# Opening of an attention and phase-mixing kernel: side work of batch 0 and the scores of batch 1 are held until batch 0's sines are rounded

## The chip, the core and the metric

The kernel runs on one core of a Trainium2 chip. Five engines work side by side, each with its own queue of instructions in a fixed order: TensorE (PE, matrix products into PSUM), VectorE (DVE), ScalarE (ACT), GpSimd (POOL) and SyncE (SP), which here issues the DMAs. They wait for each other through semaphores. The metric is the device time of one execution in microseconds, the median of several runs. The time before is 597.99 us.

## The reference

Eight batches go through a masked attention and then through a layer that mixes positions and channels:

```python
scores = scale * np.matmul(q, k.transpose(0, 1, 3, 2))
scores = np.where(masks[None, :, :, :], scores, -1000000000.0)
attn = softmax(scores)                     # with 1e-9 in the divisor
x = concat_heads(np.matmul(attn, v))       # (8, 576, 512)
theta = x @ w_theta
zr, zi = x * np.cos(theta), x * np.sin(theta)
y = einsum('ts,bsd->btd', w_tok_r, zr) + einsum('ts,bsd->btd', w_tok_i, zi)
u = x + y
out = u + np.maximum(u @ w_ch, 0.0)
```

There are 8 heads of width 64 and 576 positions. Half of the heads look back over a window of 32 positions, the other half over every fourth of 128 positions. The weight matrices are shared by all batches.

## The kernel before

**What is computed in which form.** Heads are taken in four pairs per batch, (b, pr). Since each query sees few keys, the scores of a pair are nine blocks of 128 x 64 (`scores`, L438), made by 36 small matmuls in two groups of PSUM bank `s`, which has two buffers. The softmax runs along the 64 columns: DVE takes maxima, ACT takes exponentials, POOL multiplies by the reciprocal of the sum (L507). The matrix P (two buffers from batch 1 on) is transposed in `turn` (L511, eight DVE instructions a pair) and multiplied with V in `pv` (L600). V comes in two parts, `va` with two buffers and `vb` with one.

Large products are made from rounded halves: a float is split into a high part (a cast, on ACT or DVE) and a low part (a subtraction on POOL), and three products of halves replace one. That holds for the weights (`split`, L344), for x (`x_split`), for the products with sine and cosine (`zsplit`, L630; names `zh`, `zl`) and for u (`residual`, L774). The weights come from the host as 64-bit words and are unpacked first (`unpack`, L308: a clamp on DVE, two passes on ACT of which one may go to DVE, and a combination on DVE).

**The stages of a batch.** `theta` makes five tiles of 128 rows of theta (the last, with 64 rows, first), `trig` (L722) turns each into sine and cosine, multiplies with x and rounds, which gives nine pairs `zh`, `zl` (NK = 9). `token` (L790) adds nine times three products with the token weights; there are 4 x 2 such units, first those with weights g = 0 (`wtkh`, `wtkl`, loaded early), then g = 1 (`late_wt_a`, `late_wt_b`, the late token weights). `chan` (L821) does the channel product, another eight units.

**The order.** From batch 1 on, `phase` (L841) interleaves the units of one batch with the scores, products and theta of the next by a table. The opening, from the loads of batch 0 to the end of its units, is written by a planner instead (class `Order`). Each piece of work is a generator that yields an engine with a cost, or an event to wait for; the planner keeps a clock for each engine and gives a free engine to the ready piece with the lowest rank (`RANK`, L33). The order in which the pieces come out is the order of instructions in each engine's queue, and it is fixed (`pin`). The events of the planner only shape that order; what an instruction really waits for on the chip is its data and its buffers.

The pieces that matter here: `theta_split` (L358) splits the theta weights, which batch 0 uses whole and batch 1 in halves; `token_weights(1, n, ...)` (L365) unpacks and splits the five late token weights, in buffers (`u3`, `xh0` to `xh3`) that are free between other uses; `chan_weights` (L381) does so for the channel weights, in `xh2` and `xh3` after them; `scores(1, pr)` are the scores of batch 1, of which pairs 2 and 3 wait for the event `sin0` (all sines and cosines of batch 0 have been taken). Exponential and sine need different tables of ACT, so a change between them loads a table.

`on_pe` (L412) says for which pairs the mask is added by PE (a matmul of a bf16 identity with the mask, `mask_on_pe`); then DVE takes row maxima of the masked scores (`row_max`) and ACT takes exponentials straight from PSUM (L482). For the others, among them pairs 0 and 1 of batch 1, DVE adds the mask and takes the maximum in nine instructions (`mask_scores`, L406), writing the masked scores to P, and ACT takes exponentials from there (L501).

Of the kernel before, what the change touches and what calls it, by code (L numbers as in the profile page):

```python
# [30 lines left out]
LATE = ("u3", "xh1", "xh2", "xh3", "xh0")  # L31
LATE2 = ("xh2", "xh3", "xh2", "xh3")
RANK = dict(load=6.64, scores0=1.09, flip=0.01, pv0=1.13, pair=.21, theta_unpack=1.54, theta0=5.3, trig0=2.41,  # L33
            token_early=2.55, theta_split=6.42, token_late=6.75, chan=2.1, units=2.95, evacuate=4.49,
            scores1=4.02, scores2=7.3, pv1=8.0, theta1=5.96, trig1=7.42)
STS = (4, 0, 1, 2, 3)

# [14 lines left out]
NK = 9  # L52
# [7 lines left out]
class Order:  # L60
# [13 lines left out]
    def pin(self, ins):  # L74
        if self.live:
            self.tc.keep_in_program_order(ins)

    def signal(self, event):
        self.events[event] = self.now

    def go(self, gen, rank=None):
        if not self.live:
            for _ in gen:
                pass
            return
        self.serial += 1
        t = [self.rank if rank is None else rank, self.serial, self.now, gen, None, 0.0]
        self.tasks.append(t)
        self.advance(t)
# [39 lines left out]
def dve(n):  # L129
    return 67 + 1.04 * n  # L130


def dve2(n):
    return 67 + 0.52 * n


def act(n):
    return 95 + 0.83 * n
# [6 lines left out]
def dma(n):  # L145
    return 128 * 4 * n / 360.0
# [3 lines left out]
def build(ctx, tc, qT, kT, vw, wth, wtk, wch, maskb, ident, identb, outT):  # L150
# [14 lines left out]
    pin, go, signal = od.pin, od.go, od.signal  # L165

    def pe(ins):
        tc.keep_in_program_order(ins)
# [17 lines left out]
    def take(tag, bufs, n=None):  # L186
        n = reserve(tag) if n is None else n
        if od.live:
            if n >= bufs:
                yield None, ("free", tag, n - bufs)  # L190
            if n:
                yield None, ("got", tag, n - 1)
            signal(("got", tag, n))
        return n
# [113 lines left out]
    def unpack(src, sz, name, stage, early, n, key):  # L308

        tag = None  # L310
        if stage is None:
            st = hp.tile([128, 2 * DM], F32R, tag=f"wc{n}", name=f"st_{name}{n}")
        else:
            tag = stage
            yield from take(tag[0], 1, tag[1])
            st = hp.tile([128, 2, S], F32R, tag=tag[0], name=f"st_{name}{n}").rearrange("p a b -> p (a b)")
        raw = st[:, :2 * sz].bitcast(U32)
        yield "DMA", dma(2 * sz)
        if len(src.shape) == 3:
            pin(nc.sync.dma_start(raw.rearrange("p (c b) -> p c b", c=src.shape[1]), src.bitcast(U32)))  # L320
        else:
            pin(nc.sync.dma_start(raw, src.bitcast(U32)))
        signal(("raw", name, n))
        yield None, ("raw", name, n)
        pair = raw.rearrange("p (a b) -> p a b", b=2)
        Ci, Ti = pair[:, :, 1], pair[:, :, 0]
        C, T = Ci.bitcast(F32), Ti.bitcast(F32)
        yield "DVE", dve2(sz)
        pin(nc.vector.tensor_scalar(C, C, W_MAX, -W_MAX, op0=ALU.min, op1=ALU.max))
        yield "ACT", act(sz)  # L330
        pin(nc.scalar.activation(C, C, AF.Prelu, scale=2.0 ** -112, alpha=-2.0 ** 32))
        if early and n % 2 == 0:
            yield "DVE", dve2(sz)
            pin(nc.vector.tensor_scalar(Ti, Ti, 29, None, op0=ALU.logical_shift_right))
        else:
            yield "ACT", act(sz)
            pin(nc.scalar.activation(Ti, Ti, AF.Copy, scale=2.0 ** -29, bias=-0.5))
        yield "DVE", dve(sz)
        pin(nc.vector.scalar_tensor_tensor(out=Ti, in0=Ci, scalar=3, in1=Ti,
                                           op0=ALU.logical_shift_left, op1=ALU.bitwise_or))  # L340
        signal(key)
        return T, tag
# [15 lines left out]
    def theta_split(c):  # L358
        for st in range(5):
            yield None, ("th0", st, c)  # L360
        wths[c] = tuple(cp.tile([128, DM], F32R, name=f"wth{h}{c}") for h in "hl")
        yield from split(wth32[c], DM, wths[c], ("wth", c))
        signal(("wc", c))
# [46 lines left out]
        signal(key)  # L410

    def on_pe(b, pr):  # L412
        return b == 0 or (b, pr) in ((1, 2), (1, 3), (2, 0), (2, 1))

    def mask_on_pe(ps, pr, g0, g1):
        n = g0
# [20 lines left out]

    def scores(b, pr):  # L438
        yield None, ("qk", b, pr)
        if b == 1 and on_pe(b, pr):  # L440
            yield None, "sin0"
        if pr >= 1:
            yield None, ("sc", b, pr - 1)
        q, k, rqk = qks[b, pr]
        if b == 0:
            P, rp = pqs[pr].rearrange("p (a b) -> p a b", b=BW), None
        else:
            rp = yield from take("P", 2)
            P = sp.tile([128, NJ, BW], F32, tag="P", name=f"P{b}_{pr}")
        mx = sp.tile([128, NJ], F32, tag=f"mx{b == 0 and pr}", name=f"mx{b}_{pr}", bufs=1 if b == 0 else 2)  # L450
        sm = sp.tile([128, NJ], F32, tag=f"sm{b == 0 and pr}", name=f"sm{b}_{pr}", bufs=1 if b == 0 else 2)
        held = {}
        for g0, g1 in ((0, 5), (5, NJ)):
            ps, rel = yield from bank("s", f"s{b}_{pr}_{g0}")
            ps = ps[:, :(g1 - g0) * BW].rearrange("p (a b) -> p a b", b=BW)
            held[g0] = ps, rel
            masked = on_pe(b, pr)
            if masked:
                yield "PE", 150
                mask_on_pe(ps, pr, g0, g1)  # L460
            yield "PE", 162 * (g1 - g0)
            for n in range(g0, g1):
                for e in range(2):
                    qb = 2 * n + e
                    pe(nc.tensor.matmul(ps[64 * e:64 * e + 64, n - g0], q[:, qb],  # L465
                                        k[:, QB * qb:QB * qb + BW], start=not masked, stop=not masked or n == g1 - 1))
            if masked:
                go(row_max(b, ps, rel, P, mx, g0, g1, ("mask", b, pr, g0)))
            else:
                go(mask_scores(ps, rel, P, mx, pr, g0, g1, ("mask", b, pr, g0)))  # L470
        signal(("sc", b, pr))
        if b == 0:
            give(f"u{pr}", 0)
        else:
            give("qk", rqk)
            go(load_qk(b * NP + pr + 2), RANK["load"])
        if b and on_pe(b, pr):
            for g0, (ps, rel) in held.items():
                yield None, ("mask", b, pr, g0)
                yield "ACT", 335 * ps.shape[1]  # L480
                for n in range(ps.shape[1]):
                    table(nc.scalar.activation(P[:, g0 + n], ps[:, n], AF.Exp, bias=mx[:, g0 + n:g0 + n + 1],  # L482
                                               scale=SCALE, accum_out=sm[:, g0 + n:g0 + n + 1]))
                give(*rel)
        else:
            for g0 in (0, 5):
                yield None, ("mask", b, pr, g0)
        if b == 0:
            yield "ACT", act(S)
            table(nc.scalar.activation(P, P, AF.Exp, scale=SCALE))  # L490
            yield "DVE", dve(S)
            pin(nc.vector.tensor_reduce(sm, P, op=ALU.add, axis=mybir.AxisListType.X))
        elif not on_pe(b, pr):
            yield "DVE", 67
            pin(nc.vector.tensor_scalar(mx, mx, -SCALE, None, op0=ALU.mult))  # L495
            if b == 1:
                yield None, "sin0"
            for n0 in range(0, NJ, 3):
                yield "ACT", 720
                for n in range(n0, n0 + 3):  # L500
                    table(nc.scalar.activation(P[:, n], P[:, n], AF.Exp, bias=mx[:, n:n + 1], scale=SCALE,  # L501
                                               accum_out=sm[:, n:n + 1]))
        yield "DVE", 200
        pin(nc.vector.tensor_scalar(sm, sm, 1e-9, None, op0=ALU.add))
        pin(nc.vector.reciprocal(sm, sm))
        yield "POOL", 1110
        pin(nc.gpsimd.tensor_tensor(P, P, sm.unsqueeze(2).to_broadcast([128, NJ, BW]), op=ALU.mult))  # L507
        probs[b, pr] = P, rp
        signal(("P", b, pr))
# [363 lines left out]
    def units(b):  # L873
        for f, i, g in UNITS:
            yield from f(b, i, g)

    def thetas(b):
        for st in STS:
            yield from theta(b, st)
            go(trig(b, st), RANK["trig1"])  # L880

    def sins(b):
        for st in STS:
            yield None, ("sin", b, st)
        signal("sin" + str(b))
# [33 lines left out]
    for n in range(NC):  # L919
        go(chan_weights(n, LA2[n]), RANK["chan"] + n * .01)  # L920
    go(sins(0), 0)
    go(units(0), RANK["units"])
    for p in range(NP):
        go(scores(1, p), RANK["scores1"] + p * RANK["pair"])
# [78 lines left out]
```

## Time and profile before

| | |
|---|---|
| runs, us | 596.26, 597.99, 598.92 (median 597.99) |
| profiled execution, us | 597.07 |
| its span, us | 595.3 |
| mean granted clock of PE | 0.984 |
| instructions | 14176 |
| DMA | 67.76 MB, mean 114 GB/s |

The span is the stretch from the first to the last instruction of the profiled execution; its time has a little around it. An engine's busy share is a mean over the span. A line of the timeline gives start, duration, engine, line of the kernel, operation, output and inputs, the number of merged instructions, and in brackets the time for which the engine was idle before it and what released it. A line of the groups gives the number of instructions, their busy time in us, the mean of one in ns, and the idle time before them.

Busy tenths of PE and of the clock that was granted to it, in 40 slices of the span:

```profile
PE   5997898999999999999999999999999999999997
PEclk9999599999999999999999999999999999999999
```

The page's two lines show an opening in which PE is not full, and from the sixth slice on a PE that nearly always has work.

### The profile page before, as it was taken

The numbers are of one execution on the slowest core, as the hardware profiler recorded it, in microseconds if no ns is written. First come the engines' busy times: TensorE is split into PE (matmuls) and PEld (weight loads), VectorE is DVE, ScalarE is ACT, GpSimd is POOL, SyncE is SP. The second block draws the span as 40 slices with busy tenths as digits, with TensorE's granted clock in tenths as the row PEclk, the third lists the DMA queues.
The fourth block names the chain that finished last, engine by engine and source line by source line (L and its number), as shares of the span: only waits on it lengthen the run. The fifth ranks groups of instructions, "written<-read, shape, count | busy, mean of one in ns | idle before, by whom it ended". The sixth has DMA issues, their size and how long they took to land.

```text
span 595.3 us, 14176 instructions
## 1 busy us (share of the span) xinstructions
PE 569.7 (96%) x5584; PEld 516.9 (87%) x5584; DVE 361.6 (61%) x1132; ACT 351.1 (59%) x939; POOL 222.4 (37%) x206
## 2 busy tenths in 40 slices
PE   5997898999999999999999999999999999999997
PEld 4744787979998899889998899989998899989997
DVE  3889888855765667465566567655665656445112
ACT  1498967687535955568553974468564785266110
POOL 2229854534322532326142442316324253315220
PEclk9999599999999999999999999999999999999999
DMA  8982347404650074302641054401742023001002
GB/s 303 398 339 61 121 160 246 142 1 141 182 160 3 2 241 142 101 2 89 197 139 62 1 181 151 154 1 40 231 142 73 0 81 100 1 1 53 28 1 81
DMA packets 26866, 67.76 MB, mean 114 GB/s; under 512 B 2992, under 2 KB 3248, under 8 KB 26800
## 3 DMA queue, kind: packets, MB, share of 16 engines
q1 hardware_dynamic: 26800, 66.86, 32.9%
q8 instruction: 44, 0.72, 0.5%
q14 instruction: 22, 0.18, 0.1%
HBM read 57.41 MB, written 9.44 MB: 112 GB/s over the span
## 4 chain that ended last, share of the span: by engine, by line
PE 49%; DVE 22%; ACT 21%; issue 3%; POOL 2%; DMA 2%; SPq 0%; ACTq 0%; DVEq 0%; POOLq 0%
PE y L804 27%; DVE pt L522 9%; PE c L834 8%; PE s L465 5%; ACT P L501 5%; PE o L614 4%; PE th L682 3%; ACT K L697 3%; ACT zh L641 3%; ACT g L754 2%; ACT K L695 2%; DVE P L406 2%; DVE K L702 2%; POOL P L507 2%; ACT L754 1%
## 5 line engine op out<-in xcount | busy, mean ns | idle before, releaser
L787 POOL TENSOR_TENSOR u<-x,u 128x288 fp32r<-128x288 f32 x64 | 54.9, 858 | 184.9 <-ACT u L785 162.2
L522 DVE STREAM_TRANSPOSE pt<-P 32x288 f32<-32x288 f32 x224 | 105.1, 469 | 21.1 <-POOL P L507 18.0
L834 PE MATMUL c<-u,late_wc 128*128 128x288 f32 x768 | 111.7, 296 | 0.8 <-DVE x L813 0.5
L834 PEld LDWEIGHTS c<-u,late_wc 128*128 128x128 f32 x768 | 106.2, 188 | 4.8 <-DVE x L813 2.0
L785 ACT CAST u<-x 128x288 fp32r<-128x288 f32 x64 | 27.5, 430 | 129.3 <-DVE x L782 129.3
L804 PE MATMUL y<-wtkh,zh 128*128 128x288 f32 x288 | 90.6, 315 | 1.1 <-ACT zh L641 1.1
L804 PE MATMUL y<-wtkh,zl 128*128 128x288 f32 x288 | 86.6, 301 | 3.7 <-POOL zl L643 3.7
L804 PE MATMUL y<-wtkl,zh 128*128 128x288 f32 x288 | 86.2, 299 | 0.0
L643 POOL TENSOR_TENSOR zl<-g,zh 128x512 fp32r<-128x512 f32 x40 | 52.6, 1316 | 79.1 <-ACT zh L641 66.7
L501 ACT ACTIVATE P<-P,mx 128x64 f32<-128x64 f32 x216 | 72.1, 336 | 16.8 <-DVE mx L495 16.8
L682 PE MATMUL th<-wthh,xh 128*128 128x512 f32 x224 | 76.3, 402 | 0.0
L782 DVE TENSOR_TENSOR x<-y,x 128x288 f32<-128x288 f32 x64 | 28.7, 450 | 66.8 <-PE y L804 64.0
L804 PE MATMUL y<-late_wt_b,zh 128*128 128x288 f32 x320 | 68.1, 297 | 0.0
L804 PE MATMUL y<-late_wt_a,zh 128*128 128x288 f32 x256 | 58.0, 308 | 2.7 <-DVE x L782 2.7
L804 PEld LDWEIGHTS y<-wtkh,zh 128*128 128x128 f32 x288 | 55.4, 192 | 4.8 <-ACT zh L641 2.3
L804 PEld LDWEIGHTS y<-wtkh,zl 128*128 128x128 f32 x288 | 55.3, 192 | 4.5 <-POOL zl L643 4.5
L804 PEld LDWEIGHTS y<-wtkl,zh 128*128 128x128 f32 x288 | 55.5, 193 | 0.3 <-issue 0.3
L643 POOL TENSOR_TENSOR zl<-K,zh 128x512 fp32r<-128x512 f32 x32 | 42.0, 1312 | 36.1 <-ACT zh L641 36.1
L507 POOL TENSOR_TENSOR P<-P,sm 128x576 f32<-128x576 f32 x32 | 37.5, 1172 | 43.8 <-ACT xh L590 19.3
L804 PEld LDWEIGHTS y<-late_wt_b,zh 128*128 128x128 f32 x320 | 51.4, 189 | 0.3
L682 PEld LDWEIGHTS th<-wthh,xh 128*128 128x128 f32 x224 | 42.1, 188 | 8.3
L804 PE MATMUL y<-late_wt_b,zl 128*128 128x288 f32 x160 | 47.3, 296 | 0.0
(103 smaller groups left out, 1110.0 us busy)
## 6 DMA issues: line engine op xcount, KB each, us to landing
q<-in_qT_dram SPq DMA_DIRECT2D x32, 576.0 KB, 4.2
va<-in_vw_dram SPq DMA_DIRECT2D x30, 320.0 KB, 3.2
out_dram<-x SPq DMA_DIRECT2D x32, 288.0 KB, 2.1
k<-in_kT_dram SPq DMA_DIRECT2D x28, 304.0 KB, 4.6
vb<-in_vw_dram SPq DMA_DIRECT2D x29, 256.0 KB, 3.4
st_wtk<-in_wtk_dram SPq DMA_DIRECT2D x8, 576.0 KB, 8.8
st_wth<-in_wth_dram SPq DMA_DIRECT2D x4, 512.0 KB, 9.8
st_wch<-in_wch_dram SPq DMA_DIRECT2D x4, 512.0 KB, 4.9
```

Source lines behind the costliest of these rows:

```text
L465: pe(nc.tensor.matmul(ps[64 * e:64 * e + 64, n - g0], q[:, qb], k[:, QB * qb:QB * qb + BW], start=not masked, stop=not masked or n == g1 - 1))
L501: table(nc.scalar.activation(P[:, n], P[:, n], AF.Exp, bias=mx[:, n:n + 1], scale=SCALE, accum_out=sm[:, n:n + 1]))
L507: pin(nc.gpsimd.tensor_tensor(P, P, sm.unsqueeze(2).to_broadcast([128, NJ, BW]), op=ALU.mult))
L522: pin(nc.vector.transpose(pmats[b, pr][k0:k0 + QB, :, hh, QB * e:QB * e + QB], P[p0:p0 + QB, :, QB * o:QB * o + QB]))
L614: pe(nc.tensor.matmul(ps[64 * hh:64 * hh + 64, BW * j:BW * j + BW], v[:, 64 * hh:64 * hh + 64], pmats[b, pr][:, j, hh], start=True, stop=T ...
L643: pin(nc.gpsimd.tensor_tensor(lo, z, hi.bitcast(F32), op=ALU.subtract))
L682: pe(nc.tensor.matmul(pt, l, r, start=(n == 0), stop=(n == 3 * NC - 1)))
L782: pin(nc.vector.tensor_tensor(x[:, ts], ps, x[:, ts], op=ALU.add))
L785: pin(nc.scalar.copy(uh[b, d][:, ts], x[:, ts]))
L787: pin(nc.gpsimd.tensor_tensor(ul[b, d][:, ts], x[:, ts], uh[b, d][:, ts].bitcast(F32), op=ALU.subtract))
L804: pe(nc.tensor.matmul(ps, l[:, cs], r, start=(n == 0), stop=(n == 3 * NK - 1)))
L834: pe(nc.tensor.matmul(ps, l[:, cs], r[:, ts], start=(n == 0), stop=(n == 3 * NC - 1)))
```

## The change

A new event `z0` is signalled when all nine rounded pairs z of batch 0 are there. Four things wait for it in the planner: the splits of the theta weights; the unpacking of late token weights and of channel weights (their loads are issued as before); all scores of batch 1, where only pairs 2 and 3 waited, and for `sin0`. The rank of the late token weights goes from 6.75 to 3.9. And the masks of all pairs of batch 1 are added by PE; with that the wait for `sin0` inside the other branch of `scores` has no use any more.

```diff
-            token_early=2.55, theta_split=6.42, token_late=6.75, chan=2.1, units=2.95, evacuate=4.49,
+            token_early=2.55, theta_split=6.42, token_late=3.9, chan=2.1, units=2.95, evacuate=4.49,
...
         signal(("raw", name, n))
         yield None, ("raw", name, n)
+        if not early:
+            yield None, "z0"
...
     def theta_split(c):
         for st in range(5):
             yield None, ("th0", st, c)
+        yield None, "z0"
...
     def on_pe(b, pr):
-        return b == 0 or (b, pr) in ((1, 2), (1, 3), (2, 0), (2, 1))
+        return b < 2 or (b, pr) in ((2, 0), (2, 1))
...
     def scores(b, pr):
         yield None, ("qk", b, pr)
-        if b == 1 and on_pe(b, pr):
-            yield None, "sin0"
+        if b == 1:
+            yield None, "z0"
...
             pin(nc.vector.tensor_scalar(mx, mx, -SCALE, None, op0=ALU.mult))
-            if b == 1:
-                yield None, "sin0"
...
+    def sines_first(b):
+        for kt in range(NK):
+            yield None, ("z", b, kt)
+        signal("z" + str(b))
...
     go(sins(0), 0)
+    go(sines_first(0), 0)
```

## The prediction

> **What bounds the kernel now.** I read the page's busy rows first, then busy time by stretch, then each engine's instructions in order of time around the opening.
>
> ```profile
> PE 569.7 (96%) x5584; PEld 516.9 (87%) x5584; DVE 361.6 (61%) x1132; ACT 351.1 (59%) x939; POOL 222.4 (37%) x206
> ```
> ```profile
> 0.00:66.50 66.50, 52.09 (x608) 34.02 (x608) 49.64 (x124) 43.23 (x84) 29.71 (x27) 0.93 0.74 274
> 66.50:142.40 75.90, 72.52 (x682) 65.59 (x683) 58.25 (x126) 56.91 (x164) 40.49 (x35) 0.94 0.34 117
> 142.40:595.30 452.90, 445.07 (x4297) 417.25 (x4296) 253.68 (x883) 250.98 (x693) 152.22 (x146) 1.00 0.27 90
> ```
>
> The columns of the second fence are length, then busy time of PE, PE's weight load, DVE, ACT and POOL, granted clock, DMA share and GB/s. After 142.4 us PE is busy 445.07 of 452.90 us, and the change touches nothing there. So the change is worth whatever it moves the moment at which PE starts on batch 1's token units, and everything before that decides. Two moments matter:
>
> ```profile
> 66.52 0.61 PE L804 MATMUL y<-wtkh,zl 128*128 128x288 f32 x1 [0.80 <-POOL zl L643]
> 101.25 0.30 PE L421 MATMUL s<-mskb,idb 128*128 128x64 bf16 x2 [1.95 <-ACT P L482]
> 114.49 0.39 PE L687 MATMUL th<-wthh,xh 128*128 128x512 f32 x1
> 143.54 0.40 PE L804 MATMUL y<-wtkh,zh 128*128 128x288 f32 x1
> 147.10 0.29 PE L804 MATMUL y<-wtkh,zl 128*128 128x288 f32 x1
> ```
>
> At 66.52 PE gets the last rounded half of batch 0's z (POOL's `zl`) and from there has work without end; that is the event the change calls `z0`. From 143.54 to 147.10 runs batch 1's first token unit, 27 matmuls, 0.137 us apart. Between lie only 75.90 - 72.52 = 3.4 us of idle PE, 1.95 of them in one wait. The clock adds losses:
>
> ```profile
> 66.50:71.25 4.75, 4.73 (x20) 4.73 (x20) 2.52 (x9) 4.75 (x23) 4.12 (x4) 0.50 0.00 0
> 99.00:106.00 7.00, 5.05 (x50) 4.20 (x50) 5.50 (x16) 4.60 (x22) 1.96 (x3) 0.76 0.84 273
> ```
>
> PE ran 4.75 us at half clock just after 66.5 (2.4 us lost), and after the 1.95 us wait again: a granted 0.76 over 7 us is 1.7 us lost.
>
> **The change, part by part.**
>
> *1. z0 comes earlier.* What now sits between batch 0's sines and that moment, and will wait:
>
> ```profile
> L406 DVE CUSTOM_DVE_ANT_0 P<-s,mskb 128x64 f32<-128x64 f32 x18 | 2.9, 214 | 0.0
> L329 DVE TENSOR_SCALAR st_wtk<-st_wtk 128x576 f32<-128x576 f32 (+1 forms) x6 | 6.0, 996 | 0.0
> L643 POOL TENSOR_TENSOR zl<-g,zh 128x512 fp32r<-128x512 f32 x5 | 7.4, 1486 | 5.5 <-DVE zh L638 5.5
> L643 POOL TENSOR_TENSOR zl<-K,zh 128x512 fp32r<-128x512 f32 x4 | 5.8, 1458 | 0.6 <-ACT zh L641 0.6
> L349 POOL TENSOR_TENSOR wthl<-st_wth,wthh 128x512 fp32r<-128x512 f32 x3 | 4.0, 1323 | 0.0
> ```
> ```profile
> 45.21 3.40 POOL L643 TENSOR_TENSOR zl<-g,zh 128x512 fp32r<-128x512 f32 x2 [4.38 <-DVE zh L638]
> 48.58 1.50 POOL L349 TENSOR_TENSOR wtkl<-st_wtk,wtkh 128x576 fp32r<-128x576 f32 x1
> 53.31 1.44 POOL L349 TENSOR_TENSOR wtkl<-st_wtk,wtkh 128x576 fp32r<-128x576 f32 x1
> 56.16 1.03 POOL L349 TENSOR_TENSOR wtkl<-st_wtk,wtkh 128x288 fp32r<-128x288 f32 x1
> 64.89 1.57 POOL L643 TENSOR_TENSOR zl<-K,zh 128x512 fp32r<-128x512 f32 x1 [0.61 <-ACT zh L641]
> ```
> ```profile
> 61.74 1.28 ACT L501 ACT_TABLE_LOAD   x1
> 64.19 0.62 ACT L641 CAST zh<-K 128x512 fp32r<-128x512 f32 x1
> ```
> ```profile
> L347 ACT CAST wthh<-st_wth 128x512 fp32r<-128x512 f32 x4 | 2.6, 650 | 0.0
> ```
>
> The first fence is groups between 40 and 66.5 us (busy us, mean ns). On ACT the last rounding (64.19) follows a table load and three exponentials of batch 1, 64.19 - 61.74 = 2.45 us, and the four theta casts (2.6 us) further up. On DVE the masks go, and with them late-token clamps (some of the six L329, mean 996 ns). Both engines then finish earlier than POOL, which becomes the limit: from 45.21 on it must do nine `zl` (7.4 + 5.8 = 13.2 us) and three early `wtkl` (1.50 + 1.44 + 1.03 = 4.0 us), and without the theta splits this ends at 45.21 + 17.2 = 62.4 us. It ends at 64.89 + 1.57 = 66.46 now. So the gain is at most 4.1 us by this queue. If only the two `wthl` ahead of the last `zl` count (2 x 1.32 = 2.6 us), it is 2.6; if the order changes otherwise it could be 0. I take 3.8, near the full queue, since POOL idles only tenths between its pieces there. The theta matmuls feeding the sines may come some tenths earlier too, as a score group leaves PE's queue; I count nothing for it.
>
> *2. Two pairs of scores move past z0.* Scores of (1,0) and (1,1) run on PE before 62 us today, where PE waits anyway, so they are free. After the change they are issued after z0 inside the stretch that PE fills. The price of one pair, from a pair already there:
>
> ```profile
> 76.44 0.80 PE L465 MATMUL s<-k,q 128*64 128x64 f32 x20
> 77.17 0.40 PE L804 MATMUL y<-wtkh,zh 128*128 128x288 f32 x1
> 78.36 0.69 PE L465 MATMUL s<-k,q 128*64 128x64 f32 x16
> 78.97 0.40 PE L804 MATMUL y<-wtkh,zh 128*128 128x288 f32 x1
> ```
>
> The starts give 0.73 and 0.61 us, 1.34 a pair. Masks (three instructions a pair for these pairs, matmuls of the kind at 101.25) and the four switches between kinds I estimate at 0.3, so 1.65 a pair and **3.3 us** for both. The bounds are 2.7 (nothing beside the scores) and 4.5 (part of it at half clock). This eats nearly all of part 1.
>
> *3. DVE and ACT after z0.* The 18 masked reductions (2.9 us with waits, on DVE) are replaced by two row maxima and negations a pair. Groups from 66.5 to 115.6 us:
>
> ```profile
> L427 DVE TENSOR_REDUCE mx<-s 128x5 f32<-128x320 f32 (+1 forms) x8 | 3.6, 455 | 1.8 <-PE s L465 1.7
> L435 DVE TENSOR_SCALAR mx<-mx 128x5 f32<-128x5 f32 (+1 forms) x8 | 3.2, 394 | 0.2
> ```
>
> That is four of each at 0.455 and 0.394: 3.4 us of DVE now past z0, with the clamps beside it. `z0` also stands in front of the late token weights, whose rank drops from 6.75 to 3.9, ahead of scores (4.02) and evacuation (4.49). So ACT does 4.5 chunks of two unpacking passes and a cast, 13.5 x 0.63 = 8.5 us, before batch 1's exponentials; the 0.63 is an estimate from the spacing of ACT's full-width passes, near the last cast's 0.62. Then come the table load (1.28) and nine exponentials (about 3 us). Pair (1,0) is normalised at about 62.7 + 13.5 = 76 us:
>
> ```profile
> 68.42 1.15 POOL L507 TENSOR_TENSOR P<-P,sm 128x576 f32<-128x576 f32 x1 [0.62 <-DVE sm L505]
> 99.61 0.96 DVE L522 STREAM_TRANSPOSE pt<-P 32x288 f32<-32x288 f32 x2
> 98.09 1.60 SPq L322 DMA_DIRECT2D st_wch<-in_wch_dram  x2
> 100.76 0.36 SPq L247 DMA_DIRECT2D vb<-in_vw_dram  x1
> 107.63 0.80 PE L614 MATMUL o<-pt,va 128*64 128x64 f32 x20
> ```
>
> Today it is 68.42, so attention of batch 1 starts **7.5 us later**. Behind it queue, through two P buffers, the next pairs, and then theta of batch 1 at 114.49. But there is slack on this path: the last pair's transposes end at 100.57, and its product starts only at 107.63, because SP issued the second half of its V at 100.76 behind two channel-weight loads (98.09). With late token weights rounded first, their buffers free early, the channel weights are loaded early, and this blockage of about 7 us should go. The late work now woven into 70 to 89 us is out of the way too. I cost part 3 at 0: 7.5 us late at the head against 7 us of slack and less interleaved work. If the cover is gone, rival C is the price.
>
> *4. Stalls.* The 1.95 us wait at 101.25 and its slow clock (1.7) stand for 3.7 us. PE's order is fixed by the planner, and a stall arises wherever a score of the next pair stands in front of token matmuls while its bank or buffer is still held. Removing channel weights from that place helps; two more pairs with the same banks hurt. Bounds: 0 to -5.1 (all 3.4 us of idle and 1.7), and a new one of this size is possible (+3.7). I take a third of 3.7 off, **-1.2**, nearer to no change as the mechanism remains.
>
> *The clock after z0.* Emptier PE queues before z0 may keep the clock low; it is already 0.50 in the row 66.50 to 71.25, so I keep the 2.4 us. [...]
>
> *Sum:* -3.8 + 3.3 + 0 - 1.2 = **-1.7 us**. The profiled execution took 597.07 us (span 595.3 and 1.8 around it): 595.4. The median shown, 597.99, is 0.9 higher; the forecast on it is 597.99 - 1.7 = **596.3**.
>
> **Rivals.**
>
> *B, all stalls go.* With PE dense from z0 to batch 1: -3.8 + 3.3 - 5.1 = -5.6, **592.4 us**. For it: DVE's and ACT's late work comes in one block first, so PE's scores later find their banks free. Against it: it needs theta of batch 1 to start earlier too. Its chain from 114.49 ends with the last `zl`:
>
> ```profile
> 143.05 1.28 POOL L643 TENSOR_TENSOR zl<-K,zh 128x512 fp32r<-128x512 f32 x1
> ```
>
> That is 29.8 us at 144.33, and the token unit that starts at 143.54 needs it only at its 19th matmul, 18 x 0.137 = 2.5 us in. Slack is 143.54 + 2.5 - 144.33 = 1.7 us, so theta must start 4 us earlier for B.
>
> *C, slower: batch 1's attention becomes the bound.* One place: the first pair's exponentials behind 8.5 us of late-weight passes on ACT. If only 2.5 of the 7.5 us delay is recovered, theta starts at 119.5, and batch 1's token unit waits 5 - 1.7 = 3.3 us: **601.3 us**. It decides from a theta start later than 114.49 + 1.7 = 116.2 us. For it: DVE is busy 58.25 of 75.90 us there and near its limit up to 115 us. Against it: the V blockage above.
>
> *D, z0 does not move enough.* If only POOL's two `wthl` count, -2.6 + 3.3 = +0.7 with stalls unchanged: **598.7 us**. For it: the last `zl` is a chain through theta, two table passes, a product and a rounding, which waits for PE too.
>
> **How the numbers follow.** Forecast 0.40, B 0.22, C 0.20, D 0.18. About 0.5%, 3 us here, is what a measurement of this kernel can tell from no change. B is faster by more than that; of the forecast's share, whose own range is 593.5 to 599, I give 0.13 to it as well: faster 0.35. C is slower in most of its outcomes: 0.17. The rest, 0.48, is the same. The range, 591.5 to 601.3, takes in B and most of C and leaves out stalls worse than these; the unknown stall (-5.1 to +3.7) sets both ends.
>
> **What would show it.** Right: the last `zl` of batch 0 ends near 62.7 us; two more groups of 36 score matmuls (L465) lie between token matmuls after it; the first product with P of batch 1 comes several us later than today, the last one earlier than 107.63; theta of batch 1 starts between 107 and 116 us; batch 1's token units start near 141.8. Wrong: `zl` still ending past 65, PE idle by more than 5 us between z0 and the first token unit of batch 1, or a difference that arises after that unit, where I count none.

## The result, and the profile after

The changed kernel takes **612.1 us** (median of 610.65 to 614.3), the kernel before 597.73 in the same comparison: a ratio of 1.0244, 95% interval 1.0211 to 1.0277. The forecast was 596.3 with a range up to 601.3; the time is 10.8 us above that range, on the side of rival C.

The profiled execution has a span of 610.6 us, 15.3 more than before. Busy time by stretch of the changed kernel (length, PE, PE's weight load, DVE, ACT, POOL, granted clock, DMA, GB/s):

```profile
0.00:66.50 66.50, 52.12 (x563) 33.76 (x563) 47.29 (x85) 40.33 (x66) 27.91 (x25) 0.91 0.67 246
66.50:142.40 75.90, 66.33 (x688) 59.12 (x688) 64.68 (x126) 51.70 (x167) 36.73 (x31) 0.96 0.42 138
```

In the second stretch PE is busy 66.33 us where it was 72.52, and DVE 64.68 where it was 58.25. PE waits more while DVE works more. The moments that the prediction named, in the changed kernel's order of time on POOL and PE:

```profile
62.14 1.42 POOL L644 TENSOR_TENSOR zl<-K,zh 128x512 fp32r<-128x512 f32 x1
80.09 1.34 POOL L508 TENSOR_TENSOR P<-P,sm 128x576 f32<-128x576 f32 x1
108.84 1.15 POOL L508 TENSOR_TENSOR P<-P,sm 128x576 f32<-128x576 f32 x1 [4.58 <-ACT xh L591]
158.60 1.27 POOL L644 TENSOR_TENSOR zl<-K,zh 128x512 fp32r<-128x512 f32 x1 [3.32 <-ACT zh L642]
```
```profile
118.55 0.80 PE L615 MATMUL o<-pt,va 128*64 128x64 f32 x20
125.50 0.39 PE L688 MATMUL th<-wthh,xh 128*128 128x512 f32 x1
151.65 0.40 PE L805 MATMUL y<-wtkh,zh 128*128 128x288 f32 x1
158.57 0.61 PE L805 MATMUL y<-wtkh,zh 128*128 128x288 f32 x1 [4.28 <-ACT zh L642]
```

`z0` does come earlier: the last `zl` of batch 0 ends at 62.14 + 1.42 = 63.56 instead of 66.46. Everything behind it is later. The last rounding of batch 1's z ends at 158.60 + 1.27 = 159.87 instead of 144.33, which is 15.5 us, and the span grows by 15.3. **The end of that rounding sets the time of the changed kernel.** From it to the end of the span pass 450.7 us here and 451.0 before. The first matmul that needs it is the 21st of the token unit. It came 2.0 us after the rounding's end before, so PE's own queue was the limit by that little; now it waits for the rounding (before, then after):

```profile
146.30 0.29 PE L804 MATMUL y<-wtkh,zl 128*128 128x288 f32 x1
```
```profile
159.92 0.61 PE L805 MATMUL y<-wtkh,zl 128*128 128x288 f32 x1 [0.49 <-POOL zl L644]
```

The 15.5 us divide at four events, each a start in the profiles (normalisations are POOL's P lines; V products are PE's `o` lines, pairs counted within batch 1):

| stretch | before | after | difference |
|---|---|---|---|
| normalisation of pair (1,0) starts | 68.42 | 80.09 | +11.7 |
| from there to normalisation of (1,3) | 24.35 | 28.75 | +4.4 |
| from there to V product of (1,3) | 14.86 | 9.71 | -5.1 |
| from there to theta of batch 1 | 6.86 | 6.95 | +0.1 |
| from there to the last `zl` of batch 1 | 29.84 | 34.37 | +4.5 |

(24.35 is 92.77 - 68.42, with the fourth P line of before:)

```profile
92.77 1.15 POOL L507 TENSOR_TENSOR P<-P,sm 128x576 f32<-128x576 f32 x1 [1.95 <-DVE sm L505]
```

The last row of the table has a cause of its own. ACT of the changed kernel, in order of time:

```profile
153.32 0.62 ACT L642 CAST zh<-g 128x512 fp32r<-128x512 f32 x1
153.96 1.28 ACT L502 ACT_TABLE_LOAD   x1
155.26 0.35 ACT L502 ACTIVATE P<-P,mx 128x64 f32<-128x64 f32 x1
...
157.92 0.60 ACT L642 CAST zh<-K 128x512 fp32r<-128x512 f32 x1
```

A table load and eight of the nine exponentials of pair (2,2) stand ahead of batch 1's last rounding. These belong to `phase`, after the planner's part, where the exponentials are not pinned and the scheduler may place them. The token unit waits 4.28 us for that cast.

For the first three rows, the busy time between `z0` and the first theta matmul of batch 1, before and then after, is:

```profile
66.46:114.49 48.03, 45.64 (x520) 41.92 (x521) 40.72 (x95) 37.05 (x133) 29.05 (x27) 0.91 0.51 170
```
```profile
63.56:125.50 61.94, 53.37 (x619) 47.63 (x620) 55.19 (x106) 43.03 (x146) 32.29 (x29) 0.93 0.49 161
```

PE has 7.7 us more work there and is idle 8.6 us instead of 2.4. DVE is busy 55.19 us instead of 40.72, with only 11 more instructions.

### The profile page after: what moved, and what is told of

Same layout as the page of the kernel before. It is cut to its first block, busy times and chain, and to the rows that moved or that the text cites. A ratio compares the mean times of both kernels' runs of the same rounds, so it can differ in the third digit from the quotient of the medians.

```text
span 610.6 us, 14156 instructions
## 1 busy us (share of the span) xinstructions
PE 574.2 (94%) x5590; PEld 519.2 (85%) x5590; DVE 371.6 (61%) x1102; ACT 352.8 (58%) x939; POOL 222.1 (36%) x206
## 4 chain that ended last, share of the span: by engine, by line
PE 46%; DVE 23%; ACT 21%; POOL 3%; issue 3%; DMA 2%; SPq 1%; ACTq 0%; DVEq 0%; POOLq 0%
PE y L805 24%; DVE pt L523 9%; PE c L835 8%; ACT P L502 5%; PE o L615 4%; PE s L468 4%; PE th L683 3%; ACT zh L642 3%; ACT K L698 3%; ACT g L755 2%; ACT K L696 2%; DVE P L409 2%; DVE K L703 2%; POOL P L508 2%; DVE xh L597 1%
## 5 line engine op out<-in xcount | busy, mean ns | idle before, releaser
L502 ACT ACTIVATE P<-P,mx 128x64 f32<-128x64 f32 x198 | 66.0, 335 | 20.9 <-DVE mx L498 20.8
```

## The experiments

All were profiled and timed beside the kernel before, which had medians from 597.8 to 598.3. Times below are medians. Theory 1 at the start: two separate losses, the late head of batch 1's attention and the misplaced exponentials.

**Exponentials of (2,2) in written order.**

```diff
-                    table(nc.scalar.activation(P[:, n], ...
+                    i = nc.scalar.activation(P[:, n], ...
...
+                    table(i)
+                    if (b, pr) == (2, 2):
+                        pe(i)
```

> The changed kernel with one thing held: the nine exponentials of pair (2,2) keep the written order on ACT, behind the last rounded cosine product of batch 1. Theory 1 (two separate losses: a late start of batch 1's theta, and a stall of 4.28 us plus slow clock where the token unit waits behind a table load and eight exponentials): 612.1 minus 4 to 7, so 605 to 608. Rival (the stall only shows time that is lost anyway, since the token unit would wait for theta's chain): 611 to 613.

Measured: 608.89, between the two ranges. The cast now precedes the table load, and the last `zl` ends at 154.63, 31.0 us after theta's start (123.65) instead of 34.4. Theta itself starts 1.9 us earlier in this profile, but the edit names nothing ahead of it. The stall is a real loss, worth 3.2 us by the medians where theory 1 expected 4 at least; the token unit still waits 1.35 us for the last `zl`. Later runs on the changed kernel keep this pin where they say so.

**Rank of the late token weights back.**

```diff
-            token_early=2.55, theta_split=6.42, token_late=3.9,
+            token_early=2.55, theta_split=6.42, token_late=6.75,
```

> The changed kernel with the rank of the late token weights back at 6.75; all waits stay. Theory 1 (the head of batch 1's attention is late because its exponentials queue on ACT behind the late-weight passes, ranked ahead): pair (1,0) is normalised 6 to 9 us earlier than at 80.1, theta of batch 1 starts near 118 instead of 126.5, time 599 to 605. Rival (the scores' own wait for z0 costs the start, whatever the rank): normalised after 78, time 608 to 613.

Measured: 605.31, just above theory 1's range. Pair (1,0) is normalised at 74.04, 6.1 us earlier, but theta starts at 122.40, only 3.1 earlier: from the last pair's normalisation (101.97) to its V product (117.14) pass 15.2 us instead of 9.7. The last cast also comes ahead of the exponentials here (30.8 us from theta to the last `zl`, not 34.4), so about 3.2 of the 6.8 us is the first experiment's gain. The rank sets the head, as theory 1 says, but moving it gives back only half of that.

**Scores and masks of batch 1 as before**, theta and late weights still held.

```diff
-        if b == 1:
-            yield None, "z0"
+        if b == 1 and on_pe(b, pr):
+            yield None, "sin0"
...
-        return b < 2 or (b, pr) in ((2, 0), (2, 1))
+        return b == 0 or (b, pr) in ((1, 2), (1, 3), (2, 0), (2, 1))
...
+            if b == 1:
+                yield None, "sin0"
```

> The changed kernel with scores and masks of batch 1 as before (pairs 0 and 1 masked by DVE, not held until z0); theta splits and late weights still wait, late rank 3.9. Theory 1: exponentials still wait behind the late passes on ACT, so most of the loss stays: 605 to 612. Rival (the scores' wait costs the start): 596 to 602.

Measured: 607.27, in theory 1's range (with the misplaced exponentials still in it). Free scores alone do not repair the kernel: (1,0) is normalised at 75.48.

**Masks of pairs (1,0) and (1,1) back on DVE**, by the part of the diff above in `on_pe` alone.

> The changed kernel with only the masks of pairs (1,0) and (1,1) back on DVE; all scores of batch 1 still wait for z0. If masks by PE cost much (row maxima and negations that DVE does slowly beside POOL, banks held until the exponentials): 603 to 608. If not: 610 to 614.

Measured: 614.51, just above the second case. Masks by PE are no part of the loss; they save 2.4 us here.

**Theta splits alone held behind z0**; all other parts of the change undone.

> The kernel before with one part of the change alone: theta splits wait for z0. Everything else as before. Theory 1 (the loss comes from late weights and scores held behind z0): z0 1 to 2.6 us earlier, batch 1's attention not later by more than 2 us, time 596 to 600. Rival (theta splits behind z0 load POOL, which holds DVE up, and that alone costs): 601 to 606.

Measured: 596.55, ratio 0.9984 (0.9967 to 1.0001): not told apart from before. It fits theory 1's time but not its reason, since `z0` is at 67.13, 0.7 later than before. The last `zl` of batch 1 ends at 144.21.

**Theta splits and late weights held, rank 6.75**, scores and masks as before.

> The kernel before with theta splits and the unpacking of late token and channel weights waiting for z0; the rank stays 6.75, scores and masks as before. Against the run with theta alone it prices the late weights' wait. Theory 1 (a fixed amount of DVE and ACT work moves out of engines that would have waited anyway, into a stretch where DVE is full): 1 to 4 us above the run with theta alone. Rival (late weights are not urgent, only their rank hurts): within 1 us of it.

Measured: 603.84, 7.3 above the run with theta alone; both theories had less. The profile shows another path than the one I had in mind. Here are PE's fourth V product, ACT ahead of theta, and theta's start:

```profile
101.64 0.57 PE L617 MATMUL o<-pt,va 128*64 128x64 f32 x12
```
```profile
116.38 0.65 ACT L349 CAST late_wc<-st_wch 128x512 fp32r<-128x512 f32 x1 [2.45 <-DVE st_wch L341]
117.86 0.43 ACT L788 CAST u<-x 128x288 fp32r<-128x288 f32 x1 [0.83 <-DVE x L785]
118.44 0.67 ACT L593 CAST xh<-x 128x576 fp32r<-128x576 f32 x1
```
```profile
121.74 0.63 PE L690 MATMUL th<-wthh,xh 128*128 128x512 f32 x1
```

Batch 1's attention is done 6.0 us earlier than before (101.64 against 107.63), and `z0` is at 61.43, the earliest of these runs. Yet theta starts 7.3 us later than before: its last input, the cast of x, stands on ACT behind a late channel-weight cast and a residual, which wait for DVE. So held weights delay theta even where scores do not.

**Late weights free, everything else held**, rank 6.75.

```diff
-        if not early:
-            yield None, "z0"
```

> The changed kernel with late weights free again (no wait, rank 6.75); theta splits and all scores of batch 1 still wait for z0, masks of batch 1 by PE. It prices the scores' wait. Theory 1 (with the late passes out of the way the head is late by 4 us at most, since nothing is ahead of its exponentials on ACT): 600 to 604. Rival (waiting scores alone delay every later pair by the whole head): 604 to 608.

Measured: 606.78, the rival's range. (1,0) is normalised at 76.16, 7.7 us later than before although no late pass is held, and theta starts at 124.90, 48.7 us later; before, that stretch is 46.1, so a late head is carried to theta whole. Held scores (with their masks by PE) cost 10.2 us over theta alone, held weights 7.3, both at rank 6.75 cost 605.31 - 596.55 = 8.8. They do not add up: both delay the same event.

**Negation of the row maxima on ACT**, with the pin.

```diff
-            yield "DVE", 170
-            pin(nc.vector.tensor_scalar(mx[:, g0:g1], mx[:, g0:g1], -SCALE, None, op0=ALU.mult))
+            yield "ACT", 200
+            pin(nc.scalar.activation(mx[:, g0:g1], mx[:, g0:g1], AF.Copy, scale=-SCALE))
```

> The changed kernel with the exponentials of (2,2) in written order (as in the run exps_behind, 608.9) and the negation of the row maxima on ACT instead of DVE. If DVE is what bounds the stretch after z0, and its small instructions lose time behind running POOL instructions (6.6 us for twelve there): 602 to 606. If ACT or the waits between engines bound it: 607 to 611.

Measured: 607.92, the second case. Taking twelve negations (6.6 us) off DVE changes the time by 1.0 us, less than the runs of either kernel differ among themselves.

**Low halves of the late weights on DVE instead of POOL**, with the pin.

```diff
-        yield "POOL", pool(sz)
-        pin(nc.gpsimd.tensor_tensor(lo, T, hi.bitcast(F32), op=ALU.subtract))
+        early = key[0] == "wtk" and key[1] == 0
+        yield ("POOL", pool(sz)) if early else ("DVE", dve(sz))
+        pin((nc.gpsimd if early else nc.vector).tensor_tensor(lo, T, hi.bitcast(F32), op=ALU.subtract))
```

> The run exps_behind (608.9) with the thirteen low halves of theta, late token and channel weights subtracted on DVE instead of POOL. It takes 18.7 us of work off POOL and puts 13 x 0.65 = 8.5 us on DVE. If DVE loses more than that by standing behind POOL's instructions (about 11 us longer than their undisturbed durations after z0): 603 to 608. If DVE's own amount of work decides: 611 to 617.

Measured: 608.91, the same as with the pin alone and between the two cases. DVE got 13 more subtractions, and others of its instructions became shorter: the negations 218 ns in the mean instead of 550, the subtractions from x 667 instead of 1262 (below). The two cancel: between `z0` and theta DVE is busy 54.9 us, against 55.1 with the pin alone. So the run does not tell which of them matters.

**DVE planned 1.35 times as long**, in the planner only.

```diff
             t[4], t[5] = next(t[3])
+            if t[4] == "DVE":
+                t[5] *= 1.35
```

> The run exps_behind (608.9) with one thing altered in the planner alone: every piece on DVE is planned 1.35 times as long, near what DVE's instructions took after z0 there. No work is added or taken away; only the order of the opening differs. Theory 3 (the order is written for a DVE that is faster than the real one beside POOL, so that PE's queue holds scores whose banks are not yet free: 6.3 us of PE waits for exponentials): those waits fall below 3 us, time 602 to 606. Rival (the waits come from the amount of work after z0, in any order): 607 to 611.

Measured: 615.42, 6.5 slower than without and above both ranges. PE's waits for exponentials between `z0` and theta shrink to 1.7 us, as theory 3 said, but theta's own matmuls now wait 5.7 us for DVE. Theory 3 falls.

> The kernel before with DVE planned 1.35 times as long and the exponentials of (2,2) in written order. If the misfit of the plan costs the kernel before as well (2.3 us of such waits): 594 to 597. If its order fits by having been settled with these costs: 598 to 603.

Measured: 607.75, above both ranges. Without any wait added, another order makes the kernel before 9.5 us slower.

> The run only_theta (596.6: theta splits alone wait for z0) with DVE planned 1.35 times as long. If the waits of PE there (3.1 us between z0 and theta) come from the plan: 593 to 596. If not: 597 to 602.

Measured: 604.76, above both ranges and 8.2 above the run with theta alone.

This raised theory 4: the opening's order fits its ranks and costs, and any other order loses. Four runs test it, all with the pin; the first two alter the factor only (1.05 and 0.95, kernel before), the other two the ranks:

```diff
-            scores1=4.02, scores2=7.3, pv1=8.0, theta1=5.96, trig1=7.42)
+            scores1=4.02, scores2=8.2, pv1=5.0, theta1=5.96, trig1=7.42)
```

> The kernel before with every DVE piece planned 1.05 times as long, (2,2)'s exponentials in written order: the same work in a slightly other order, no wait added. Theory 4 (the order of the opening was settled for one set of costs and ranks, and any other order costs, so most of the change's loss is that of a disturbed order): 601 to 607. Rival (small disturbances of the plan cost little; the loss is specific to the waits for z0): 596 to 600.

> As plan_105_before with the factor 0.95. Theory 4: 601 to 607. Rival: 596 to 600.

Measured: 602.41 and 601.01. A 5% disturbance of one engine's planned costs costs the kernel before 4.1 and 2.7 us. Both are in theory 4's range, 601.01 at its lower edge.

> The run exps_behind (608.9) with other ranks: products with V and x of batch 1 at 5.0 instead of 8.0, scores of batch 2 at 8.2 instead of 7.3. Theory 4 (ranks settled without the waits; others fit better with them): 600 to 606. Rival (the waits' cost stands whatever the ranks): 607 to 612.

> The kernel before with the same two ranks altered, as the control of batch1_first. Theory 4: slower than before, 600 to 606, since its ranks fit. Rival: within 2 us of before or below it.

Measured: 608.96 and 598.81, both the rival. These ranks neither help the changed kernel nor hurt the kernel before (0.5 us), so it is not true that any other order loses.

The last two give the changed kernel, with the pin, the same 5% disturbances.

> The run exps_behind (608.9) with DVE planned 1.05 times as long: the same waits and work, a neighbouring order. If the loss is only that of an unlucky order, neighbouring orders scatter down to near the kernel before with a disturbed plan (601 to 603): 600 to 605 in one of the two runs. If the waits themselves cost, both stay within 605 to 613.

> As plan_105_after with the factor 0.95; the same two cases: 600 to 605 in one of the two runs, or both within 605 to 613.

Measured: 609.57 and 611.26, both in the waits' case. At equal disturbance the changed kernel is 7.2 and 10.3 us slower than the kernel before, and at the factor 1.35 it is 7.7 slower (615.42 against 607.75). So the waits with their rank cost 7 to 10 us beside each of these orders. How much of that is the loss of an order not settled for them, the runs do not separate: on the chip nothing waits for `z0`, the waits act only through the order, and 35% on one engine's planned costs alone took 9.5 us.

All profiled executions side by side (us; "to end" is span less the end of batch 1's last `zl`):

| run | span | z0 | (1,0) normalised | theta of batch 1 | last zl of batch 1 | to end |
|---|---|---|---|---|---|---|
| before | 595.3 | 66.46 | 68.42 | 114.49 | 144.33 | 451.0 |
| after | 610.6 | 63.56 | 80.09 | 125.50 | 159.87 | 450.7 |
| exps_behind | 605.7 | 62.61 | 78.23 | 123.65 | 154.63 | 451.1 |
| rank_back | 603.5 | 62.80 | 74.04 | 122.40 | 153.19 | 450.3 |
| scores_free | 605.1 | 62.37 | 75.48 | 120.96 | 154.28 | 450.8 |
| masks_dve | 611.6 | 64.02 | 80.49 | 129.81 | 160.74 | 450.9 |
| only_theta | 595.5 | 67.13 | 69.39 | 113.33 | 144.21 | 451.3 |
| theta_late | 601.8 | 61.43 | 66.09 | 121.74 | 151.52 | 450.3 |
| late_free | 604.7 | 64.54 | 76.16 | 124.90 | 154.57 | 450.1 |
| negate_act_behind | 606.6 | 62.64 | 79.66 | 126.56 | 154.89 | 451.7 |
| lo_dve | 605.8 | 62.52 | 76.11 | 125.78 | 154.90 | 450.9 |
| plan_dve | 611.7 | 64.04 | 79.91 | 126.38 | 160.40 | 451.3 |
| plan_dve_before | 606.1 | 66.77 | 68.98 | 124.02 | 154.90 | 451.2 |
| plan_dve_theta | 603.8 | 65.67 | 67.89 | 120.52 | 152.21 | 451.6 |
| plan_105_before | 601.9 | 67.28 | 69.03 | 120.04 | 151.39 | 450.5 |
| plan_095_before | 601.1 | 67.60 | 69.86 | 120.90 | 150.16 | 450.9 |
| batch1_first | 605.5 | 62.39 | 77.90 | 121.73 | 153.08 | 452.4 |
| batch1_first_before | 597.1 | 67.38 | 69.34 | 116.29 | 146.29 | 450.8 |
| plan_105_after | 610.0 | 63.51 | 79.08 | 126.95 | 156.98 | 453.0 |
| plan_095_after | 609.4 | 64.65 | 80.78 | 127.56 | 157.61 | 451.8 |

Over 16 us of difference in span, the last column stays between 450.1 and 453.0. An earlier `z0` does not go with a shorter span: the run with the earliest `z0` (61.43) is 6.5 us longer than before. In 14 of the 20 profiles PE is shown waiting for that last `zl`; in the others, before and only_theta among them, it is not, and the distance holds within the same bounds.

## Why the prediction was wrong, step by step

**What bounds the kernel.** The prediction took the end of the opening as PE's path from `z0` on, with batch 1's theta chain 1.7 us behind it. The chain was the right rival for the bound, and the slack about right for the kernel before (the last `zl` is needed at the 21st matmul, not the 19th, so it is 2.0 us). With the change the chain is the bound, and the earlier `z0` did not shorten it.

**1, z0.** Forecast 62.7, measured 63.56: -2.9 instead of -3.8. POOL began the nine `zl` at 46.03 instead of 45.21 and waited 1.2 us between its pieces. A size error, of no consequence here.

**2, scores past z0.** Forecast +3.3 on PE. From `z0` to batch 1's first token unit PE is busy 45.64 + 28.02 = 73.7 us before, and after the change:

```profile
125.50:151.65 26.15, 25.09 (x178) 21.93 (x176) 17.11 (x37) 18.32 (x35) 10.98 (x9) 1.00 0.10 38
```

With 53.37 that makes 78.5, so +4.8, just above its upper bound of 4.5. It does not add to the time, since PE waits more than that.

**3, DVE and ACT after z0: the step that failed.** The prediction said: "I cost part 3 at 0: 7.5 us late at the head against 7 us of slack and less interleaved work." The delay at the head was right in kind and too small: +11.7. The late passes run with waits for DVE in between (2.17 us the longest), so the table load comes only at 73.44 and the exponentials at 74.74.

```profile
73.44 1.28 ACT L485 ACT_TABLE_LOAD   x1
74.74 0.31 ACT L485 ACTIVATE P<-s,mx 128x64 f32<-128x64 f32 x1
```

But the late passes, to which the prediction put the delay down, are only a part of it. With the late weights free (late_free) the head is still 7.7 us late, because scores, maxima and exponentials of the pair now start behind `z0`:

```profile
76.16 1.15 POOL L506 TENSOR_TENSOR P<-P,sm 128x576 f32<-128x576 f32 x1 [1.49 <-ACT late_wt_b L347]
```

The slack was there too: V of the last pair no longer waits behind channel weights, and the stretch to its product shrinks by 5.1 us. SP of the changed kernel:

```profile
92.94 0.33 SPq L322 DMA_DIRECT2D st_wch<-in_wch_dram  x1
...
111.40 0.34 SPq L247 DMA_DIRECT2D vb<-in_vw_dram  x1
```

What I left out is the stretch between the first and the last pair, which I took to have "less interleaved work": it grew by 4.4 us and used up most of the slack. Why it grew stays open. It is 29.3 us with held scores and free late weights (late_free), 21.9 with held weights and scores as before (theta_late), and 30.6 with nothing held and DVE planned 5% longer (plan_105_before), against 24.4 before.

The net is +11.0 at theta instead of 0, as rival C describes it (a theta start past 116.2). Rival C had the bound right; the one place that it named is a part of the delay, and its price assumed 5 us. By its reckoning 11.0 us cost 11.0 - 1.7 = 9.3; with the 3.2 us of the first experiment that makes 12.5 of the 14.4 us that the kernel lost (612.1 - 597.73), and 1.9 us are not assigned.

**4, stalls.** Forecast -1.2. PE's idle time between `z0` and theta rose from 2.4 to 8.6 us, mostly scores waiting for banks (us in total, times, longest):

```profile
PE s L424 <- ACT P L485: 6.3, 6, 2.9
```

"Two more pairs with the same banks hurt" was the half that counted. But plan_dve shows that removing these waits is not enough: with 1.7 us of them left the time got worse.

**5, not foreseen.** The misplaced exponentials, which the first experiment prices at 3.2 us. "A difference that arises after that unit, where I count none" was named as a sign of being wrong, and it was one: from the start of batch 1's token unit to the end pass 451.8 us before and 459.0 after. With the exponentials in written order 455.9 are left: the unit still waits 1.7 us for its last halves, and after that 20 matmuls of a V product (155.81) take 1.14 us, where 20 of the same form at 116.68 took 0.80.

**Open.** How much a full search of ranks would regain with the waits kept was not tried beyond the runs above. Nor do the runs separate the price of each instruction that moved, or the waits from the order that comes of them; they show that held scores and held weights each delay theta of batch 1.

## What to carry to other kernels

Work placed early into engines that wait anyway is free only there; holding it back to speed up the event they wait for pays only if that event sets the end, so find the event whose distance to the end stays constant over variants before pulling at another, and look whether its reader waits for it. A slack found at one place of a pipeline pays for a delay at its head only if the places between have room as well. Where an order is written out by a planner, time a disturbed plan of the unchanged kernel as a control: here 5% on one engine's costs was worth 2.7 to 4.1 us and 35% was worth 9.5, and a part of that size may be in the effect of any change to such a kernel.

## What the hardware showed unexpectedly

Two small DVE instructions of the changed kernel lasted until the POOL instruction that they met had ended: 1.25 and 1.28 us, against 0.17 alone. DVE and POOL, in order of time:

```profile
95.92 1.25 DVE L438 TENSOR_SCALAR mx<-mx 128x4 f32<-128x4 f32 x1
...
103.01 1.28 DVE L438 TENSOR_SCALAR mx<-mx 128x5 f32<-128x5 f32 x1
...
106.74 0.17 DVE L438 TENSOR_SCALAR mx<-mx 128x4 f32<-128x4 f32 x1
```
```profile
95.86 1.28 POOL L351 TENSOR_TENSOR late_wc<-st_wch,late_wc 128x512 fp32r<-128x512 f32 x1
...
102.95 1.30 POOL L351 TENSOR_TENSOR late_wc<-st_wch,late_wc 128x512 fp32r<-128x512 f32 x1 [0.18 <-ACT late_wc L349]
```

A negation of 128 x 4 numbers took 0.17 us at 106.74, when POOL was idle (from 104.25 to 108.84), and 1.25 at 95.92, when POOL had started 0.06 us earlier: it ended with POOL's instruction (97.17 and 97.14). So did that of 128 x 5 at 103.01 (104.29 and 104.25). With the low halves taken off POOL the mean of the negations falls from 550 to 218 ns; the first fence shows groups of the changed kernel (63.5 to 126.5 us), the second those of lo_dve (63 to 123 us):

```profile
L438 DVE TENSOR_SCALAR mx<-mx 128x5 f32<-128x5 f32 (+1 forms) x12 | 6.6, 550 | 0.3
L597 DVE TENSOR_TENSOR xh<-x,xh 128x512 fp32r<-128x512 f32 x3 | 3.8, 1262 | 0.0
L523 DVE STREAM_TRANSPOSE pt<-P 32x288 f32<-32x288 f32 x40 | 18.8, 469 | 0.8
```
```profile
L439 DVE TENSOR_SCALAR mx<-mx 128x5 f32<-128x5 f32 (+1 forms) x11 | 2.4, 218 | 0.2
L601 DVE TENSOR_TENSOR xh<-x,xh 128x512 fp32r<-128x512 f32 x3 | 2.0, 667 | 0.0
L527 DVE STREAM_TRANSPOSE pt<-P 32x288 f32<-32x288 f32 x39 | 18.3, 469 | 1.0 <-POOL P L512 0.3
```

The subtraction `xh<-x,xh` falls from 1262 to 667 ns, and the transpose stays at 469. Why the one depends on the work on POOL and the other does not, no run shows. What the runs do show is that removing such losses need not move the time, where other work takes their place: 608.89 with the low halves on POOL and 608.91 with them on DVE.
